# Sliding-window attention feeding an MoE block: a padded last token block, fp32 loads in long runs with casts on GpSimd, row-tiled scores by head pair, and the two MoE stages interleaved

## The chip, the cores and the metric

The kernel runs on one core of a Trainium2 chip. The metric is the device time of one execution in microseconds (us); lower is better. Before the change it is 407.75 us, the median of four runs (407.3 to 408.6). The profile and the trace come from one profiled execution, whose span is a little shorter (406.9 us before), because it leaves out what surrounds the program.

A few names are used throughout. PE is TensorE's matmul stream and PEld its weight loads; DVE is VectorE, ACT is ScalarE, POOL is GpSimd; SPq and POOLq are the two queues from which DMAs are issued. The *pitch* of a matmul is the time from its start to the start of the next one. A matmul's recorded duration overlaps its neighbours, so pitch and not duration is what a matmul costs. A *visit* is a run of matmuls of one operand shape among matmuls of another. A *period* is the time between equal points of two successive blocks.

## The reference

Eight batches of eight heads, 576 tokens, head size 64. Every query sees itself and the 63 tokens before it. The result, 4608 tokens by 512, goes through two weight matrices with a hard-swish between them. All inputs and outputs are fp32.

```python
scores = q @ k.transpose(0, 1, 3, 2) / sqrt(64)
rel = pos[:, None] - pos[None, :]
scores = where((rel >= 0) & (rel < 64), scores, -1e9)
attn = softmax(scores);  x = (attn @ v) -> [4608, 512]
h = x @ w_in                      # [4608, 2048]
g = h * clip(h + 3, 0, 6) / 6
out = g @ w_out                   # [4608, 512]
```

## The kernel before

Each batch of 576 tokens is four blocks of 128 tokens and one of 64. Attention of batch b and MoE of earlier tokens share one PE order: attention code calls `weave()` before its matmuls (those of P·V excepted), and each call takes one MoE instruction from a queue. MoE works on nine blocks of 512 tokens; stage 1 (`hT`, 64 matmuls) and stage 2 (`acc`, 64 matmuls) of a block have 512 columns each, so there are 1152 of them.

Loads are DMAs that cast fp32 to bf16 on the way. Each run is one head's 64 elements of one token, 256 bytes read and 128 written:

```python
nc.gpsimd.dma_start(                       # the same for k and for v
    out=qk16[:ss, 0 : H * D].rearrange("p (h d) -> p h d", h=H),
    in_=q[b, :, s0 : s0 + ss, :].rearrange("h s d -> s h d"))
```

Queries are transposed and copied, one copy per head, into a buffer whose other half is zero, so that one matmul of 384 columns gives the scores of two heads. The last token block keeps its true size of 64 (`nn`, `mq`, `nn_q`):

```python
nc.tensor.matmul(st[:nn, 0 : 2 * mq],
    lhsT=KT_b[:, g, n0 : n0 + nn], rhs=QZ_b[:, g, :, n0 : n0 + mq], ...)
# ... exp on ACT, mask multiply on DVE ...
nc.tensor.matmul(o_aug[:, qb, :],
    lhsT=pTp[:nn_q, par, qb, 0:P], rhs=V16s[qb][:nn_q, h, 0 : D + 1], ...)
```

MoE is queued stage after stage. Stage 1 needs an ACT and a DVE operation on each `hT` before that PSUM buffer is free again:

```python
while stage1_done < NTB and (stage1_done + 1) * TB <= tokens_ready:
    if stage1_done >= 1 and stage2_done < stage1_done:
        emit_moe_stage2(stage2_done); stage2_done += 1
    emit_moe_stage1(stage1_done); stage1_done += 1
# ... attention weaves the queue in; what is left over runs alone
```

The softmax here doesn't subtract the row's maximum and nothing guards it: scores larger than these inputs give would overflow.

## Time and profile before

| | before |
|---|---|
| time, median of four | 407.75 us |
| profiled span | 406.9 us |
| PE / DVE / ACT / POOL busy | 91 / 62 / 57 / 26 % |
| five steady periods (from 85.3 us to 293.4 us) | 41 to 43 us each |

The first lines are from the page of the profile of before: busy time by engine; the span in 40 slices of 10.2 us, where a digit is the busy share in tenths (PEclk: the granted TensorE clock, DMA: the busy share of the 16 DMA engines); the DMA queues (packets, MB, share of the engines' time); the shares of the chain of waits that ended last; and one group of instructions.

```profile
PE 369.2 (91%) x2325; PEld 183.2 (45%) x2368; DVE 250.5 (62%) x791; ACT 233.9 (57%) x581; POOL 106.3 (26%) x136
...
PE   1477887999999999999999999999999999999975
...
PEclk9996788999999999999999999999999999999999
DMA  9999999989692969198919950110011002002011
...
q0 software_dynamic: 115168, 18.36, 66.1%
...
PE 75%; ACT 7%; DVE 7%; DMA 5%; issue 3%; POOL 1%; ACTq 0%; POOLq 0%
...
L442 PE MATMUL acc<-wout_147,gT 128*128 128x512 bf16 x519 | 151.8, 380 | 1.5 <-DVE gT L407 1.1
```

PE is busy almost everywhere from 70 us on and it carries 75% of the chain, so it is the bound. But "91% busy" is not work at the peak: the group's 380 ns is a duration. The next lines, from the chain of waits of before (start, length, what, in us), show what a matmul costs.

```profile
213.41 1.83 PE acc L442 x8
...
254.43 1.83 PE acc L442 x8
...
312.20 0.69 ACT t_4322 L400
312.92 0.70 DVE gT L407
314.04 0.66 PE hT L387 x3
...
331.67 3.24 PE acc L442 x15
```

Fifteen `acc` matmuls take 3.24 us, a pitch of 0.216 us. All 1152 need 249 us. The same point comes back after 41.0 us (213.41 and 254.43). At 312 us, in the part without attention, PE's order in the trace is four `hT` matmuls, one `acc`, four `hT` and so on, and the chain goes ACT, DVE, PE: these five matmuls (1.08 us by the pitch) do not cover the 0.69 and 0.70 us of ACT and DVE, and stage 1 waits for its own PSUM buffers.

Now the timeline of PE in before (start, duration, engine, line, operation, count), at the end of one head's P·V:

```profile
211.30 0.20 PE L298 MATMUL o_aug<-Vr_138,pTr_128 128*128 128x65 bf16 x1
211.34 0.19 PE L307 MATMUL o_aug<-Vr_137,pTr_128 128*128 128x65 bf16 x1
211.46 0.20 PE L298 MATMUL o_aug<-Vr_139,pTr_128 64*128 64x65 bf16 x1
211.59 0.20 PE L307 MATMUL o_aug<-Vr_138,pTr_128 128*128 128x65 bf16 x1
```

Only the third of these has 64 rows. It starts 0.12 us after its predecessor, and its successor 0.13 us after it; matmuls of 128 rows beside it start 0.03 to 0.04 us apart. So one small odd-shaped matmul costs some 0.2 us.

### The profile page before, as it was taken

The page shows a single profiled execution, that of the slowest core. Times are in us where ns is not written, and L with a number is a line of the kernel's source. Part 1 is how long each engine was busy: PE and PEld are TensorE (multiplying, and loading weights), DVE is VectorE, ACT ScalarE, POOL GpSimd, SP SyncE. Part 2 cuts the span into 40 slices and gives each one's busy share as a digit, 9 for nine tenths or more (in the row PEclk, how much of TensorE's full clock was granted, in tenths as well). Part 3 has the DMA queues.
Part 4 walks back from the last instruction along what each step waited for, and adds up shares of the span by engine and source line. Part 5 has one row for each costly group of instructions (what it writes and reads, how often), then busy time and mean ns, then how long its engine had stood idle before and what let it go on. Part 6 is the DMA issues. An engine that isn't in the chain of part 4 may idle for free.

```text
span 406.9 us, 6550 instructions
## 1 busy us (share of the span) xinstructions
PE 369.2 (91%) x2325; PEld 183.2 (45%) x2368; DVE 250.5 (62%) x791; ACT 233.9 (57%) x581; POOL 106.3 (26%) x136
## 2 busy tenths in 40 slices
PE   1477887999999999999999999999999999999975
PEld 1234453445544554455445544554454334334332
DVE  7678666877777677866686677667753541532510
ACT  2375654785588457846784578457835543543521
POOL 9995554346131514151415120000000000000000
PEclk9996788999999999999999999999999999999999
DMA  9999999989692969198919950110011002002011
GB/s 81 135 143 202 138 114 184 87 71 144 67 58 37 117 69 59 30 96 98 60 19 104 101 34 25 36 44 3 3 50 53 0 26 79 0 27 79 0 52 52
DMA packets 120384, 28.21 MB, mean 69 GB/s; under 512 B 113184, under 2 KB 115232, under 8 KB 120352
## 3 DMA queue, kind: packets, MB, share of 16 engines
q0 software_dynamic: 115168, 18.36, 66.1%
q1 hardware_dynamic: 5184, 9.44, 6.2%
q8 instruction: 18, 0.29, 0.3%
q14 instruction: 14, 0.11, 0.1%
HBM read 36.70 MB, written 9.44 MB: 113 GB/s over the span
## 4 chain that ended last, share of the span: by engine, by line
PE 75%; ACT 7%; DVE 7%; DMA 5%; issue 3%; POOL 1%; ACTq 0%; POOLq 0%
PE acc L442 27%; PE hT L387 18%; PE hT L375 7%; PE st L262 6%; PE o_aug L298 4%; PE o_aug L307 3%; DVE gT L407 3%; PE xp L350 3%; DMA wout_147<-in_moe_w_out_dram 3%; PE xpq L211 3%; PE xpk L235 2%; PE acc L430 2%; ACT osb L455 1%; DMA Vr_134<-in_v_dram 1%; DMA qk_148<-in_k_dram 1%
## 5 line engine op out<-in xcount | busy, mean ns | idle before, releaser
L442 PE MATMUL acc<-wout_147,gT 128*128 128x512 bf16 x519 | 151.8, 380 | 1.5 <-DVE gT L407 1.1
L387 PE MATMUL hT<-xT_all,win_146 128*128 128x512 bf16 x411 | 119.0, 384 | 0.9 <-issue 0.2
L442 PEld LDWEIGHTS <-gT 128*128 128x128 bf16 x540 | 50.5, 97 | 58.7 <-issue 7.5
L387 PEld LDWEIGHTS <-win_146 128*128 128x128 bf16 x432 | 41.5, 98 | 49.6 <-issue 10.6
L375 PE MATMUL hT<-xT_all,win_146 128*128 128x512 bf16 x143 | 55.2, 386 | 3.4 <-DVE gT L407 3.3
L455 ACT COPY osb<-acc 128x512 f32<-128x512 f32 x36 | 21.0, 584 | 44.3 <-PE acc L442 43.4
L222 ACT COPY qz_132<-xpq 64x128 bf16<-64x128 bf16 (+1 forms) x80 | 19.2, 245 | 31.4 <-DVE qz_132 L227 18.6
L222 ACT COPY qz_133<-xpq 64x128 bf16<-64x128 bf16 (+1 forms) x80 | 19.2, 247 | 24.8 <-DVE qz_133 L227 18.2
L357 ACT COPY xT_all<-xp 128x256 bf16<-128x256 bf16 (+1 forms) x80 | 25.8, 363 | 7.2 <-PE xp L350 6.5
L262 PE MATMUL st<-qz_132,KT_b 128*128 128x384 bf16 (+1 forms) x80 | 24.0, 330 | 3.6 <-DVE qz_132 L227 2.2
L331 DVE TENSOR_TENSOR opg<-o_aug,rec 128x256 bf16<-128x256 f32 x64 | 26.5, 415 | 0.1
L262 PE MATMUL st<-qz_133,KT_b 128*128 128x384 bf16 (+1 forms) x80 | 24.8, 328 | 1.9 <-DVE qz_133 L227 0.7
L262 PEld LDWEIGHTS <-KT_b 128*128 128x128 bf16 (+1 forms) x160 | 15.9, 104 | 18.9 <-issue 12.3
L350 PE MATMUL xp<-ident_123,opg 128*128 128x128 bf16 (+1 forms) x160 | 22.4, 218 | 2.2 <-DVE KT_b L240 0.7
L227 DVE COPY qz_132<-xpq 64x128 bf16<-64x128 bf16 (+1 forms) x80 | 17.1, 221 | 11.4 <-ACT qz_132 L222 9.6
L227 DVE COPY qz_133<-xpq 64x128 bf16<-64x128 bf16 (+1 forms) x80 | 17.3, 221 | 10.1 <-ACT qz_133 L222 8.6
L322 DVE RECIPROCAL rec<-o_aug 128x4 f32<-128x4 f32 x64 | 11.6, 181 | 18.6 <-PE o_aug L307 17.5
L350 PEld LDWEIGHTS <-opg 128*128 128x128 bf16 (+1 forms) x160 | 13.7, 98 | 18.1 <-DVE opg L331 6.2
L375 PEld LDWEIGHTS <-win_146 128*128 128x128 bf16 x144 | 14.2, 99 | 13.9 <-issue 2.3
L240 DVE COPY KT_b<-xpk 128x512 bf16<-128x512 bf16 (+1 forms) x40 | 15.9, 396 | 7.3 <-PE xpk L235 6.2
L430 PE MATMUL acc<-wout_147,gT 128*128 128x512 bf16 x36 | 13.6, 378 | 4.8 <-ACT osb L455 2.5
L339 DVE TENSOR_SCALAR opg<-o_aug,rec 64x64 bf16<-64x64 f32 x64 | 17.3, 270 | 0.7
(754 smaller groups left out, 684.0 us busy)
## 6 DMA issues: line engine op xcount, KB each, us to landing
out_dram<-osb SPq DMA_DIRECT2D x36, 256.0 KB, 2.0
win_146<-in_moe_w_in_dram POOLq DMA_DIRECT2D x4, 512.0 KB, 10.0
wout_147<-in_moe_w_out_dram POOLq DMA_DIRECT2D x2, 1024.0 KB, 12.9
Vr_135<-in_v_dram POOLq DMA_DIRECT2D x4, 128.0 KB, 4.8
Vr_134<-in_v_dram POOLq DMA_DIRECT2D x3, 128.0 KB, 4.6
Vr_136<-in_v_dram POOLq DMA_DIRECT2D x3, 128.0 KB, 4.8
Vr_137<-in_v_dram POOLq DMA_DIRECT2D x3, 128.0 KB, 5.2
Vr_140<-in_v_dram POOLq DMA_DIRECT2D x3, 128.0 KB, 5.8
```

The source lines that it names most:

```text
L222: nc.scalar.copy(out=QZ_b[pl:ph, g, half, s0 : s0 + ss], in_=xpq[pl:ph, j, :ss],)
L227: nc.vector.tensor_copy(out=QZ_b[pl:ph, g, half, s0 : s0 + ss], in_=xpq[pl:ph, j, :ss],)
L262: nc.tensor.matmul(st[:nn, 0 : 2 * mq], lhsT=KT_b[:, g, n0 : n0 + nn], rhs=QZ_b[:, g, :, n0 : n0 + mq], start=True, stop=True,)
L331: nc.vector.tensor_tensor(out=opg[:, 0:nfull, hq, :], in0=o_aug[:, 0:nfull, 0:D], in1=rec[:, 0:nfull].unsqueeze(2).to_broadcast([P, nfull, ...
L339: nc.vector.tensor_scalar_mul(out=opg[:mm, qb, hq, :], in0=o_aug[:mm, qb, 0:D], scalar1=rec[:mm, qb : qb + 1],)
L350: nc.tensor.transpose(out=xp[:, j, :mm], in_=opg[:mm, qb, 2 * j : 2 * j + 2, :].rearrange("p a d -> p (a d)"), identity=ident16[:mm, :mm],)
L357: nc.scalar.copy(out=xT_all[:, gb : gb + HC // 2, t_lo : t_lo + mm], in_=xp[:, 0 : HC // 2, :mm],)
L375: nc.tensor.matmul(hT[:, :tn], lhsT=win16[:, 0, fc * P : (fc + 1) * P], rhs=xT_all[:, 0, t0 : t0 + tn], start=True, stop=(NG == 1),)
L387: nc.tensor.matmul(state["hT"][:, :tn], lhsT=win16[:, g, fc * P : (fc + 1) * P], rhs=xT_all[:, g, t0 : t0 + tn], start=False, stop=(g == N ...
L430: nc.tensor.matmul(acc[:uu, :], lhsT=gT[:, 0, tsub * P : tsub * P + uu], rhs=wout16[:, 0, :], start=True, stop=(NFC == 1),)
L442: nc.tensor.matmul(state["acc"][:uu, :], lhsT=gT[:, fc, tsub * P : tsub * P + uu], rhs=wout16[:, fc, :], start=False, stop=(fc == NFC - 1),)
L455: nc.scalar.copy(out=osb[:uu, :], in_=acc[:uu, :])
```

## The change

The intent: long DMA runs for q and k, no half-zero operands, fewer and wider copies, no 64-row leftovers, and stages 1 and 2 interleaved so that each hides the other's waits. The core of the diff, with cuts:

```diff
-            nc.gpsimd.dma_start(out=qk16[...], in_=q[b, :, s0 : s0 + ss, :]...)   # casts, 256 B read
+                nc.sync.dma_start(                                  # fp32, runs of R*D*4 = 1536 B
+                    out=dst[:NP, h0 : h0 + step, :],
+                    in_=src[b, h0 : h0 + step].rearrange("h (p j) d -> p h (j d)", j=R))
+    # vst: fp32 as well, 256 B runs, on the same queue
+                if not first: nc.gpsimd.tensor_copy(out=o_ap, in_=i_ap)   # cast on GpSimd
+                elif i == 0:  nc.vector.tensor_copy(out=o_ap, in_=i_ap)   # batch 0: q on DVE
+                else:         nc.scalar.copy(out=o_ap, in_=i_ap)          #          k on ACT
+        nc.gpsimd.tensor_copy(out=V[...], in_=vst[...])
+    # w_in is issued at once, beside batch 0; w_out beside batch 1

-        # QZ_b: queries copied per head beside zeros, one matmul of 384 columns for two heads
+                    for h in range(2):                               # two row tiles of 64
+                        nc.tensor.matmul(st[:, h, off : off + w],
+                            lhsT=KT[h * D : (h + 1) * D, kb * P : (kb + 1) * P],
+                            rhs=QT[h * D : (h + 1) * D, kb * P : kb * P + w], ...)
-        lhsT=pTp[:nn_q, par, qb, 0:P], rhs=V16s[qb][:nn_q, h, 0 : D + 1]
+        lhsT=pT[:, h, qb, 0:P],        rhs=V[:, qb, 2 * g + h, :]    # padded to 128 rows
+    # one mask multiply for a pair of heads, 128x1920, in place of five

-    emit_moe_stage2(stage2_done); emit_moe_stage1(stage1_done)       # one after the other
+        main = zipped(s1(T), s2(T - 1) if T else None)               # 4 of one, 4 of the other
+        weave(main, 32 if T else 16, side, 24)                       # attention spread evenly
```

## The prediction

> **What bounds the kernel now.** TensorE. The page shows PE busy 91% of 406.9 us, DVE 62%, ACT 57%; the chain of waits is 75% PE. That busy time overlaps (380 ns per 512-column matmul); in the tail of the chain 15 such matmuls take 3.24 us, a pitch of 0.216 us. The 1152 MoE matmuls need 249 us. From pitches in the timeline near 205 us (transpose 0.056, 384-column score 0.16, P·V 0.035 to 0.04) attention needs about 8.6 us a batch, 69 in all. So 318 us of pitch stand in a span of 407; 89 are lost:
> - Start: MoE runs in earnest only from 64 us. The chain shows a 10.8 us wait for w_out; the DMA engines are 90% busy for most of the first 140 us (113,184 packets under 512 B).
> - Middle: the same point recurs every 41.0 to 41.6 us (long runs of `acc` at 213.4, 254.4, 296.1), 5 us above 27.6 + 8.6. The timeline shows gaps of 0.1 us on entering and on leaving matmuls of 64 rows or columns, 0.2 us a visit.
> - Tail: from 311 us 3 stage-1 blocks and 3.2 stage-2 blocks take 96 us, pitch 86; where stage 1 runs alone, the chain alternates PE 0.66, ACT 0.70, DVE 0.70.
>
> **The change, costed (my estimates from those durations).**
> - Scores: 384 half-zero columns become two 64-row matmuls of 192. If the pair runs concurrently, as the Trainium skill, "TensorEngine Tiling (Array Packing)", § Key Properties says of tiles, 2.8 us a batch become 1.7. The same section says that a mode change drains the array; eight visits cost 1.6. Padding removes other 64-row visits. A batch: 27.6 + 8.1 + 1.6 = 37.3 without waits.
> - New waits: one buffer each for transposes, scores, output. The PE order leaves 0.86 to 1.08 us of MoE matmuls between transposes of q and of k, and between score halves; drain, handshakes and queueing take about 1.4. Eight stalls: 3 to 4 us. Casts on GpSimd, perhaps 10 us a batch, can block the mask multiply: the Trainium skill, "SBUF — State Buffer", § "SBUF: two separate sides", calls the shared port an exclusive lock. No trace here shows it yet. Period: about 40.5 us, hardly below 41.
> - ACT loses 160 query copies (38 us), DVE as many (34 us), both gain wider drains; ACT stays near 225 us, DVE falls to 200. Neither binds.
> - Loads: 256-byte runs become 1536-byte for q and k; v stays at 256 bytes, behind them and beside w_in. First V at 25 to 30 us (before: 15), attention 0 done near 42, the first period (stage 1 of block 0 with attention 1) near 68.
> - Interleaved stages cover the PE-ACT-DVE chain. Tail: two periods of 28.5 us and a last stage 2 of 17.
>
> **Sum.** 68 + 6 x 40.5 + 57 + 17 = 385 us. Range 367 to 402. Faster by over 2%: 0.79; within 2%: 0.15; slower: 0.06. The gain is mostly the tail (22 us), little the steady part.
>
> **What would show each step.** Start: first P·V waiting for V or its cast. Steady: equal points 38 to 43 us apart; paired scores near 0.085 us each; PE waits on DVE for QT and on ACT for exp. Tail: pitch near 0.22 us from two periods before the end. DMA share far below 0.9 after 80 us. Mask multiplies near 1.2 us; much longer means blocked.
>
> **What would make it wrong.** Mask multiplies blocked for several us (period 43 or more, about 400 us); row pairs not concurrent (+10 us); fewer stalls than I count and a faster start (period 38, 365 us or less).

## More of the kernel before

Last, the windows view of before: busy time of each engine in two stretches, then clock, DMA share and GB/s. (The DMA share counts overlapping packets, so it can pass 1.)

```profile
core 0: us, PE busy (x) PEld busy (x) DVE busy (x) ACT busy (x) POOL busy (x), PEclk, DMA share, GB/s
0.00:85.30 85.30, 61.24 (x422) 33.59 (x427) 63.31 (x233) 47.55 (x144) 53.39 (x73) 0.88 1.72 129
...
169.90:211.10 41.20, 40.47 (x282) 20.82 (x285) 28.95 (x95) 27.88 (x72) 12.59 (x16) 1.00 0.78 69
```

The first is the start: PE has work in only 61 of 85 us, while the DMA engines are full. Its clock is to be read with care: the view counts time without a clock record as full speed, and the records begin only at 26.2 us. The first q/k transposes, of 128 columns, start 0.107 us apart, later ones about 0.055, so half clock came before the records too. The second is one of five steady periods, in which PE hardly pauses. After 293 us comes the end, 113.5 us, in which attention runs out. The rest of the text speaks of these three parts.

## The result, and the profile after

The kernel after takes 376.71 us, the median of four runs: 374.35, 374.68, 378.91 and 378.74. The two longer ones had a mean granted clock of 0.973 and the two shorter of 1.0. (The clock alone does not explain them: later the fastest of four runs of this kernel, 372.79 us, was the only one with a lower clock, 0.986.) Executions over 1.5% slower than the fastest of the same kernel are left out of the means. A ratio is the mean time of one kernel's runs over that of the other's in the same rounds, so it is not quite the ratio of the medians. Here it is 0.9236, with a 95% interval of 0.9179 to 0.9293: faster. The prediction was 385 us, 367 to 402.

The page of the profile of after (slices are 9.3 us here):

```profile
PE 333.0 (89%) x2544; PEld 168.6 (45%) x2592; DVE 194.6 (52%) x285; ACT 214.6 (58%) x345; POOL 74.7 (20%) x54
...
PE   0156789999999999999999999999999999999985
...
PEclk9999999999999999999999999999999999999999
DMA  8999999999999148605760000000000010110111
...
q1 hardware_dynamic: 55424, 37.76, 43.2%
```

Two readings. PE starts later than before (0 1 5 6 against 1 4 7 7), and the DMA engines are still busy until about 121 us, although the share of the two queues together fell from 72.3% (66.1 and 6.2) to 50.0% (43.2 and 6.8). The row of 9s for the clock is no measurement in the first slices: the records begin at 55.7 us. Before that the q/k transposes of 96 columns start 0.080 us apart, after it 0.042, so by the pitches TensorE ran at half clock until then. The chain of waits of after has the same kind of recurring point, now 36.8 us apart:

```profile
210.00 0.97 PE acc L296 x4
...
246.78 0.97 PE acc L296 x4
```

The timeline of PE in after, at the end of a P·V and at one visit of paired scores:

```profile
214.68 0.19 PE L231 MATMUL o<-V_152,pT_145 128*128 128x65 bf16 x1
214.71 0.19 PE L236 MATMUL o<-V_152,pT_145 128*128 128x65 bf16 x1
214.74 1.03 PE L296 MATMUL acc<-wout_111,gT 128*128 128x512 bf16 x3
215.70 0.34 PE L201 MATMUL st<-QT_139,KT_141 64*128 64x192 bf16 x4
```

P·V now keeps its 0.03 us from the first matmul to the last. The windows view of after, in the stretches that answer to those of before, with the same columns:

```profile
0.00:85.40 85.40, 55.42 (x494) 31.21 (x502) 44.61 (x67) 44.13 (x70) 40.52 (x36) 1.00 1.11 215
...
158.40:195.20 36.80, 36.33 (x304) 18.55 (x309) 21.95 (x32) 24.53 (x42) 7.88 (x4) 1.00 0.51 125
```

PE has less to do in a period than before (36.33 us busy against 40.47) and, as before, hardly pauses. (The 1.00 of the first line is not measured before 55.7 us, as said.) Equal points were fixed for this account: the copies of `acc` out of PSUM, of which every fourth begins a new block of 512 tokens. Working out the differences of their times in the two traces:

| part | before, us | after, us | difference |
|---|---|---|---|
| start, to the first such copy | 85.3 | 85.4 | 0 |
| five steady periods | 208.1 | 183.4 | -24.7 |
| from there to the end of the span | 113.5 | 103.8 | -9.7 |

So the start gained nothing, the steady part most. The work done at such a point is not quite equal: after has written 100 pieces of `gT` where before has written 96 (16 matmuls, 3.5 us), and before is a little ahead in transposes and scores. By the pitches the net is 1 to 2 us at both points, so start and end are good to about 2 us. To see inside a period, each start-to-start interval on PE was put down to the kind of the earlier matmul, over three batches (us a batch):

| | MoE, both stages | q/k transposes | scores | P·V | output transposes | sum |
|---|---|---|---|---|---|---|
| before | 28.7 | 2.99 | 3.39 | 4.62 | 1.42 | 41.1 |
| after | 28.4 | 2.27 | 2.40 | 2.40 | 1.34 | 36.8 |

P·V is half of the saving of 4.4 us. (Some matmul records are missing, 5 or 6 of 128 MoE matmuls a batch in both traces; their time goes to the kind recorded before them.)

Who waits for whom on PE in after, over the whole run (us in total, times, longest):

```profile
PE tr L178 <- DVE ident L110: 15.8, 1, 15.8
PE o L231 <- POOL V_149 L165: 3.1, 1, 3.1
PE acc L296 <- ACT osb L303: 3.0, 4, 0.9
```

The same view limited to 158 to 269 us, three whole periods, is empty: PE waits for nothing there. In before, from 170 to 293 us, it holds only 0.5 us, so there too the longer period lay in the pitches and not in waits. The first wait of after is the start. The timeline of after shows it (in brackets: the idle time just before, and what ended it):

```profile
5.21 0.28 POOL masks.py:199 TENSOR_SCALAR_AFFINE_SELECT ident_116<-ident_116 128x128 f32<-128x128 f32 x1
...
15.03 0.56 DVE L162 CAST qn<-qst 96x768 bf16<-96x768 f32 x1 [1.70 <-DMA qst<-in_q_dram]
15.51 0.21 DVE L110 CAST ident<-ident_116 128x128 bf16<-128x128 f32 x1
15.78 0.64 PE L178 MATMUL tr<-ident,qn 96*128 96x96 bf16 x6 [15.78 <-DVE ident L110]
...
27.14 1.89 POOL L165 CAST V_149<-vst 128x2048 bf16<-128x2048 f32 x1 [12.10 <-DMA vst<-in_v_dram]
...
29.09 0.27 PE L231 MATMUL o<-V_149,pT_143 128*128 128x65 bf16 x2 [3.06 <-POOL V_149 L165]
```

The identity matrix is made by 5.5 us, but its cast to bf16 stands on DVE behind four q casts that each wait for a load. All transposes wait for it until 15.78 us. P·V of batch 0 then waits for the cast of V, whose loads compete with w_in.

### The profile page after: what moved, and what is told of

Read it like the earlier page. It is cut to its first block, busy times and chain, and to the rows that moved or that the text cites. A ratio compares the mean times of both kernels' runs of the same rounds, so it can differ in the third digit from the quotient of the medians.

```text
span 372.6 us, 6265 instructions
## 1 busy us (share of the span) xinstructions
PE 333.0 (89%) x2544; PEld 168.6 (45%) x2592; DVE 194.6 (52%) x285; ACT 214.6 (58%) x345; POOL 74.7 (20%) x54
## 3 DMA queue, kind: packets, MB, share of 16 engines
q1 hardware_dynamic: 55424, 37.76, 43.2%
## 4 chain that ended last, share of the span: by engine, by line
PE 51%; ACT 2%; DVE 2%; DMA 1%; another core or an unknown queue 1%; issue 1%; SPq 1%; ACTq 0%
PE acc L296 23%; PE hT L280 20%; PE st L201 2%; PE tr L178 2%; DMA vst<-in_v_dram 1%; PE o L231 1%; PE tr L255 1%; PE o L236 1%; ACT osb L303 1%; DVE pT_145 L219 1%; ACT pT_145 L208 0%; SPq L81 0%; DVE QT_131 L187 0%; DVE pT_147 L219 0%
## 5 line engine op out<-in xcount | busy, mean ns | idle before, releaser
L280 PE MATMUL hT<-xT,win_110 128*128 128x512 bf16 x545 | 152.2, 386 | 3.7 <-ACT xT L260 1.8
L296 PE MATMUL acc<-wout_111,gT 128*128 128x512 bf16 x559 | 146.4, 379 | 3.7 <-ACT osb L303 3.0
L160 POOL CAST qn<-qst 96x3072 bf16<-96x3072 f32 x7 | 19.4, 2778 | 74.4 <-issue 56.9
L178 PE MATMUL tr<-ident,qn 96*128 96x96 bf16 x192 | 14.9, 219 | 16.7 <-DVE ident L110 15.8
L245 DVE TENSOR_TENSOR opg<-o,rec 128x640 bf16<-128x640 f32 x32 | 26.4, 825 | 1.1
L260 ACT COPY xT<-tr 128x576 bf16<-128x576 bf16 x32 | 20.6, 642 | 9.0 <-PE tr L255 8.5
L208 ACT ACTIVATE pT_147<-st 128x768 bf16<-128x768 f32 x20 | 16.1, 808 | 11.5 <-PE st L201 11.5
L208 ACT ACTIVATE pT_143<-st 128x768 bf16<-128x768 f32 x22 | 17.8, 808 | 7.1 <-PE st L201 7.1
L208 ACT ACTIVATE pT_145<-st 128x768 bf16<-128x768 f32 x22 | 17.7, 806 | 5.5 <-PE st L201 5.5
L160 POOL CAST kn<-kst 96x3072 bf16<-96x3072 f32 x7 | 19.2, 2740 | 6.6 <-DMA kst<-in_k_dram 6.6
L219 DVE TENSOR_TENSOR pT_143<-pT_143,mask 128x1920 bf16<-128x1920 bf16 x11 | 13.2, 1199 | 9.8 <-ACT pT_143 L214 9.8
L219 DVE TENSOR_TENSOR pT_145<-pT_145,mask 128x1920 bf16<-128x1920 bf16 x11 | 13.2, 1196 | 9.5 <-ACT pT_145 L214 9.5
L255 PE MATMUL tr<-ident,opg 128*128 128x128 bf16 x160 | 15.5, 231 | 2.0 <-DVE opg L245 1.2
L219 DVE TENSOR_TENSOR pT_147<-pT_147,mask 128x1920 bf16<-128x1920 bf16 x10 | 12.5, 1253 | 8.5 <-ACT pT_147 L214 8.5
```

Source lines behind the costliest of these rows:

```text
L160: nc.gpsimd.tensor_copy(out=o_ap, in_=i_ap)
L178: nc.tensor.transpose(out=tr[:, j * NP : (j + 1) * NP], in_=src[:NP, j, 2 * g : 2 * g + 2, :].rearrange("p h d -> p (h d)"), identity=iden ...
L208: nc.scalar.activation(out=pT[:, :, kbs[0] : kbs[0] + 2, 0:QW], in_=st[:, :, 0 : 2 * QW].rearrange("p h (k w) -> p h k w", k=2), func=EXP, ...
L219: nc.vector.tensor_tensor(out=pT[:, :, :, 0:QW], in0=pT[:, :, :, 0:QW], in1=mask[:].rearrange("p (h k) w -> p h k w", h=2), op=MULT,)
L245: nc.vector.tensor_tensor(out=opg[:].rearrange("p k h d -> p h k d"), in0=ov[:, :, :, 0:D], in1=rec[:].unsqueeze(3).to_broadcast([P, 2, KB ...
L255: nc.tensor.transpose(out=tr[:, qb * P : (qb + 1) * P], in_=opg[:, qb, :, :].rearrange("p h d -> p (h d)"), identity=ident[:],)
```

## The experiments

Twelve runs were made, one of them of the kernel after again. Medians and ranges are of all runs of a kernel unless said; ratios are to the kernel before.

### Where do 4.4 us of a period come from?

The theory was that removing odd-shaped matmuls (padding) gave about half; the rivals were the interleaving of the stages and the row pairs of the scores. Each is undone alone, and the padding is also done alone in the kernel before.

**pv64**: P·V of the last block on its 64 real rows again. One mask entry is set to 1, so that the sum of a padding query isn't zero.

```diff
+                    kr = min(P, S - qb * P)
-                        ob, lhsT=pT[:, h, qb, 0:P], rhs=V[:, qb, 2 * g + h, :],
+                        ob, lhsT=pT[:kr, h, qb, 0:P], rhs=V[:kr, qb, 2 * g + h, :],
+    for hk in (KB - 1, 2 * KB - 1):
+        nc.vector.memset(mask[0:1, hk, P - 1 : P], 1.0)
```

> The changed kernel, with P.V of the last key block on the 64 real rows again instead of 128 padded ones (8 such matmuls a batch; result stays right). Theory A (a visit of a matmul with 64 rows costs about 0.2 us of array time, and padding them away is the larger part of the shorter steady period): period up from 36.8 by 8 x 0.2 = 1.6 us, to about 38.4, the mean P.V pitch from 33 ns to 50 ns or more, total up by about 12 us. Rival B (64-row visits are harmless, P.V was slow before because of waits on its one output buffer): period stays at 36.8 within 0.3, total within 2 us.

Measured: correct, 390.78 us (389.43 to 391.65), ratio 0.9579 (0.9553 to 0.9605). The period is 38.5 us, 1.7 longer than in after, and P·V takes 3.86 us instead of 2.40. Eight visits a batch cost 1.7 us, 0.2 us each, as the gaps in the timeline of before said. Eight batches of 1.7 us are 13.6 us, and the whole run is 14 us slower than after.

**before_padded**: the kernel before with its last block padded to 128 rows and columns everywhere, zeros in the padding.

```diff
-    # last block: nn, mq, nn_q, ss = 64
+    SP = KB * P     # QZ, KT_b [.., SP], V and the last qk16 rows zero-filled
+                n0, nn = kb * P, P
+                mq = min(QW, SP - n0)
+                    nn_q = P
```

> The kernel before, with only the last block of 64 padded to 128 rows everywhere (transposes, scores, P.V, normalise), scores still the zero-padded 384 columns in the full array. Theory A (64-row and 64-column visits cost the period): period down from 41.3 to 38 to 39 us, P.V from 4.8 to about 2.6 us a batch, total down by 15 to 22 us. Rival B (row-tiled scores and wider drains made the period short): period 41 within 0.5, total within 4 us of before.

Measured: correct, 393.54 us (393.17 to 393.88), ratio 0.9639 (0.9619 to 0.9659). The period is 39.0 us, 2.2 shorter than before, with P·V at 2.39 us. More arithmetic, and almost 15 us faster than before: just under the 15 to 22 expected, and close to half the size of the whole gain, from padding alone in a kernel otherwise unchanged.

**fullrows**: scores on all 128 rows in place of two row tiles. Each head's score then sums both heads, so it is wrong; it still passed the tolerance of the comparison, which says how little that comparison sees here.

```diff
-                            lhsT=KT[h * D : (h + 1) * D, kb * P : (kb + 1) * P],
-                            rhs=QT[h * D : (h + 1) * D, kb * P : kb * P + w],
+                            lhsT=KT[:, kb * P : (kb + 1) * P],
+                            rhs=QT[:, kb * P : kb * P + w],
```

> The changed kernel with each score matmul on all 128 rows of the array instead of one head's 64 (wrong result on purpose: both heads' scores are summed; same sizes and same order). Theory A (row pairs overlap, but entering and leaving the tiled mode takes back most of it): scores go from 2.4 to about 3.1 us a batch, period 37.2 to 37.6, total up by 3 to 6 us. Rival C (row tiling is a main source of the gain): period up by over 2 us, total up by over 15 us. Rival D (mode changes cost more than the overlap saves): total goes down.

Measured: 375.38, 376.21 and 377.15 us (one slow run of 381.46 left out), ratio 0.9216 (0.9187 to 0.9245): no difference from after in time. The 3 to 6 us expected in the total did not show; after's own four runs spread by 4.6 us. With the clock below full only from 38 to 57 us, the steady periods can be read: 37.2 us, 0.4 longer, scores 3.07 us instead of 2.40. In after the two matmuls of a pair start 6 to 9 ns apart, in fullrows 82 ns, so the pairs do run side by side; still, row tiling is worth only about 0.4 us a batch, a tenth of the saving.

**apart**: stage 2 and then stage 1, one after the other, as before. This is the order of the program; in the trace PE's order is mixed in both kernels (from 327 to 342 us of apart mostly one `acc` matmul after every four of `hT`, as in the end of before).

```diff
-        main = zipped(s1(T), s2(T - 1) if T else None)
+        main = chained(s2(T - 1) if T else None, s1(T))
```

> The changed kernel with stage 2 of the block before and stage 1 of this block one after the other in each period instead of interleaved. If interleaving is what shortens the tail: the two periods without attention grow from 27.8 to 33 to 35 us each (stage 1 alone took about 19.5 us before), the steady periods grow by 0 to 2 us since attention still lies between, total up by 10 to 20 us. Rival (the tail was shortened by fewer blocks being left over, not by interleaving): total within 4 us.

Measured: correct, 391.30 us (388.11 to 394.69, with one slow run), ratio 0.9558 (0.9492 to 0.9624). The period is 38.5 us, 1.7 longer. It is not a matter of waits: over three periods PE waits 0.5 us in all. By kind, 0.9 of the 1.7 us lie in the MoE matmuls and 0.7 in the scores, whose visits are now split by MoE matmuls; why the MoE matmuls take longer was not taken apart. The three blocks after the last full period take 38.5, 30.5 and 29.4 us, where after has 34.8, 27.6 and 25.0; the 33 to 35 us expected of the two without attention did not come. The sum to the end of the span is 11 us longer, but not all of that is interleaving: at the point where it begins, after has written 100 pieces of `gT` and apart 96, and is ahead in transposes and scores, some 5 us by the pitches. That leaves some 6 us. The waits agree in kind: in the part without attention PE waits 5.0 us for `gT` and the copy of `acc` in before (311 to 391 us), 2.7 us in apart (311 to 371 us) and not at all in after (296 to 352 us). So interleaving is worth 1.7 us a period and some 6 us at the end, which is most of the 9.7 us gained there, not shown to be all.

Together: 1.7 to 2.2 for padding, 1.7 for interleaving, 0.4 for row pairs, against 4.4. The parts were measured in different surroundings, and undoing the interleaving also moved the visits of the scores, so the near-equality is not an exact sum.

### Do the casts on GpSimd block the mask multiply?

The prediction feared this. In after, 29 of the 32 mask multiplies take 1.15 to 1.16 us. Three begin while a cast runs and take 1.58, 1.62 and 2.10 us. The timeline of after shows the longest:

```profile
60.78 2.74 POOL L160 CAST qn<-qst 96x3072 bf16<-96x3072 f32 x1 [4.84 <-DMA qst<-in_q_dram]
62.44 2.10 DVE L219 TENSOR_TENSOR pT_147<-pT_147,mask 128x1920 bf16<-128x1920 bf16 x1 [0.59 <-ACT pT_147 L214]
```

The cast ends at 63.52 and the multiply at 64.54. In the other two cases the multiply too ends 1.0 us after the cast, whenever it began, so it does not run beside the cast at all. In after_again two such multiplies took 2.82 and 3.55 us, both in the start, and both end 1.0 us after the cast. After 104 us no mask multiply meets a cast in this kernel. That is luck of position, as the next run showed without being meant to.

**dense**: attention woven into the first half of each period, meant to provoke waits of transposes and scores.

```diff
-        weave(main, 32 if T else 16, side, 24)
+        weave(main, 16, side, 24)
```

> The changed kernel with all 24 attention steps of a period woven into the first half of its MoE steps instead of over the whole; the same instructions. Theory A (one-buffer handshakes of some 1.0 us are just covered by the 4 or 5 MoE matmuls between them, which is why the predicted stalls of 3 to 4 us a period did not come): with less MoE work between, stalls appear: period up by 2 to 5 us, total up by 12 to 30 us, and the profile shows waits of transposes and scores on ACT and DVE. Rival B (handshakes are too short to matter at all): period within 0.5 us, total within 4 us.

Measured: correct, 390.8 us (387.57 to 394.46, with one slow run), ratio 0.9544 (0.9497 to 0.9591). Three periods take 40.7 us. But the waits were not the expected ones (nor could they well be: PE's order still leaves four or five MoE matmuls between the transposes of q and of k). The timeline of dense:

```profile
166.40 2.74 POOL L160 CAST qn<-qst 96x3072 bf16<-96x3072 f32 x1 [24.08 <-issue]
166.99 3.17 DVE L219 TENSOR_TENSOR pT<-pT,mask 128x1920 bf16<-128x1920 bf16 x1
169.09 3.67 POOL L160 CAST kn<-kst 96x3072 bf16<-96x3072 f32 x1
170.21 0.24 PE L231 MATMUL o<-V,pT 128*128 128x65 bf16 x2 [1.95 <-DVE pT L219]
```

The multiply begins 0.6 us into the cast of q and takes 3.17 us: until the cast ends (169.14), and 1.0 us more. The cast of k that follows is held up in turn: 3.67 us in place of 2.74. PE waits 1.95 us for P·V. And then the windows view of dense, in steps of 3.4 us:

```profile
167.90:171.30 3.40, 1.35 (x24) 0.82 (x24) 3.40 (x4) 1.14 (x3) 3.40 (x2) 1.00 0.28 50
171.30:174.70 3.40, 3.33 (x17) 1.40 (x17) 1.15 (x4) 2.01 (x4) 1.46 (x1) 0.51 1.06 249
```

PE was busy only 1.35 of 3.4 us, and the granted clock in the next 3.4 us is 0.51. So each blocked multiply is paid for twice: 1.95 us of waiting and some 1.7 us of lost clock (half of 3.4 us), together about the 3.5 us by which these periods are longer than those of cd_dense below. The same happens at 130 and 212 us. In the first steady period of dense without casts (246 to 283 us) the period is 37.3 us. That suggests the cast, but the periods differ in other ways too, so it was tried.

**cd_dense**: the dense weave in the kernel `castdma` described below, which has no cast on GpSimd.

> The dense weave again, but with the loads of the version that has casting DMAs, so without any cast on GpSimd. In the dense version three periods took 40.7 us; in each a cast on GpSimd (2.74 us) ran as the mask multiply began, the multiply took 3.17 us in place of 1.16, TensorE waited 1.95 us for it and then ran at half clock for 3.4 us. The one steady period after the last cast took 37.3. Theory L (the shared port between GpSimd and VectorE is what made the dense weave dear, and the density itself costs about 0.5 us a period): all steady periods 37.0 to 37.6, all mask multiplies 1.15 to 1.2 us, no half clock after 80 us, time 364 to 369. Theory D (the density itself, attention work too close together for its own chain of scores, exponential, mask and P.V, makes TensorE wait): periods stay 39.5 to 41 with waits for the mask multiply, time 374 to 385.

Measured: correct, 367.36 us (366.73 to 368.05), ratio 0.8994 (0.8956 to 0.9032). All four steady periods from 114 us are 37.29 us, all 32 mask multiplies take 1.15 to 1.16 us, and the clock is 1.00 in every steady stretch. Between 105 and 260 us, the waits view of PE in this kernel has only short pieces that wait for no other engine; the longest in total is:

```profile
PE hT L252 <- issue: 0.8, 5, 0.2
```

Without the casts the dense weave costs 0.5 us a period (37.3 against 36.8); with them 3.9. The theory of the lock is confirmed, and that of the density itself falls. GpSimd is not idle in cd_dense: many of the multiplies run while it issues a DMA, and they too take 1.15 to 1.16 us. In the change as made the casts cost next to nothing in the steady part, because its wider spacing keeps them apart from the multiplies.

### Why did the start gain nothing?

**castdma**: the change with the loads of before: casting DMAs in 256-byte runs on one queue, in the order batch 0, w_in, batch 1, w_out; no staging buffers, no casts; the first fills moved from GpSimd to DVE.

```diff
-                nc.sync.dma_start(out=dst[:NP, h0 : h0 + step, :], in_=src[b, h0 : h0 + step]...)
+                nc.gpsimd.dma_start(out=dst[:NP, j, :, :],
+                    in_=src[b].rearrange("h (p j) d -> j p h d", j=R)[j])
-    # cast_batch(...) on DVE, ACT and GpSimd
-    for i in range(4): nc.gpsimd.dma_start(out=win16[...])     # at once, beside batch 0
+    for i in range(4): nc.gpsimd.dma_start(out=win16[...])     # behind batch 0
```

> The changed kernel with q, k and v loaded as before: casting DMAs in runs of 256 bytes, no fp32 staging, no casts on GpSimd (ring memsets moved to DVE, w_in after the first batch). Theory A (the load change shortens only the start, where the DMA engines are the limit, and the casts on GpSimd cost the steady part nothing): period stays at 36.8 within 0.3 us; the three transfers that the first period needs take about 85 us of the DMA engines instead of 59, so the first period ends 10 to 20 us later and the total is up by 10 to 20 us. Rival B (casts on GpSimd block the mask multiply): period shorter by 1 us or more. Rival C (loads do not matter): total within 4 us.

**after_again**: the kernel after, unchanged.

> The changed kernel itself, on the same chip as the three that follow, for comparison. All theories: 374 to 379 us, period 36.8 us; runs with a lower granted clock lose some 4 us in the first 80 us only.

Measured: after_again 374.98 us (372.79 to 375.93), ratio 0.9175 (0.914 to 0.921); against the expectation, its fastest run was the one with a lower clock; castdma correct, 364.15 us (363.89 to 365.91), ratio 0.8932 (0.8901 to 0.8963). The expectation for castdma was wrong by its sign: the new loads do not save 10 to 20 us, they cost 11. The steady period is the same to the hundredth, 36.78 us, so all of it is in the start. The page of castdma:

```profile
DMA  9999999999990799069905991000000000100111
...
q0 software_dynamic: 116992, 18.36, 70.2%
```

Here the DMA engines are *more* occupied (70.2% in one queue), with twice as many packets, and the kernel is faster. A busy share tells how long packets are under way, not when the bytes that someone waits for arrive. Landing times and progress, read from the traces (us; an attention is done when its last copy begins):

| | after | castdma | cd_swap | start2 |
|---|---|---|---|---|
| first work of PE | 15.8 | 5.4 | 5.4 | 9.6 |
| V of batch 0 landed | 28.3 | 21.1 | 20.2 | 17.6 |
| w_in landed | 22.9 | 31.4 | 31.6 | 41.3 |
| V of batch 1 landed | 54.4 | 44.5 | 55.3 | 48.9 |
| w_out landed | 50.7 | 56.1 | 42.0 | 64.6 |
| attention 0 done | 46.9 | 37.0 | 37.2 | 42.7 |
| attention 1 done | 78.0 | 67.5 | 76.9 | 72.3 |
| first copy of `acc` | 85.4 | 75.0 | 77.4 | 79.8 |

By about 55 us the same four things (two batches, w_in, w_out) have landed in after and in castdma, so the overall rate is the same; what differs is the order. In castdma batch 0 comes ahead of w_in and batch 1 ahead of w_out; in after they share the engines. The new loads are not slow in themselves: where batch 0 has the engines alone, its V lands at 17.6 us with them (start2) and at 21.1 without (castdma).

TensorE's clock differs too, and these runs do not tell its part from that of the waits. By the clock records and the pitches (0.080 or 0.042 us from transpose to transpose), half clock ends for good at 55.7 us in after, 53.0 in cd_swap, 50.0 in start2 and 46.1 in castdma. So a part of the differences between these kernels can be clock; how large a part is open.

**start**: the change with its fp32 loads, the cast of the identity moved to GpSimd, and the weights held back: w_in until V of batch 0 is cast, w_out until V of batch 1 is cast, each by a tiny copy that the DMA must wait for.

```diff
-    nc.vector.tensor_copy(out=ident[:], in_=ident32[:])
+    nc.gpsimd.tensor_copy(out=ident[:], in_=ident32[:])
+        nc.gpsimd.tensor_copy(out=win16[0:1, 0, 0:FF:WC], in_=V[0:1, 0, 0, 0:4])   # ahead of w_in
+        nc.gpsimd.tensor_copy(out=wout16[0:1, 0:NFC:4, 0], in_=V[0:1, 0, 0, 0:4])  # ahead of w_out
+    load_w_in(cast0[2])
+            if b == 1:
+                load_w_out(cst[2])
```

> The changed kernel with another order at the start: identity cast on GpSimd instead of behind the q casts on DVE, w_in issued only after the first V is cast, w_out only after the second V is cast. Theory A (the first 76 us are set by when the first and the second V land, which compete with w_in and w_out for the DMA engines): first V cast near 20 us instead of 27, second near 47 instead of 54, total down by 5 to 10 us. Rival B (the start is limited by the bytes or by the chain of attention itself): total within 3 us.

Measured: correct, fast runs 378.7, 379.63 and 380.23 us, ratio 0.9294 (0.9266 to 0.9322): a miss, 4 to 5 us slower than after_again. The casts of V did begin early (17.2 and 43.9 us), but w_out landed only at 57.8 to 67.9 us. Its one profiled run fell in the slow state (454.63 us), so only its order, its landings and a wait that ends with a landing are used here. In the waits view of PE:

```profile
PE acc L300 <- DMA wout<-in_moe_w_out_dram: 5.7, 1, 5.7
```

PE takes its instructions in order. The first stage-2 matmuls stand early in that order, and while they waited for w_out, the attention behind them, whose data was there, waited too.

**start2**: the same, with w_out held back only until k of batch 1 is cast.

```diff
-                load_w_out(cst[2])
+                load_w_out(cst[1])
```

> The changed kernel's fp32 loads and GpSimd casts kept; w_in behind the first batch (as in the run named start), w_out gated by the cast of the second batch's k, so that it lands near 52 to 55 us, when stage 2 needs it, and no longer at 58 to 68 as in start, where stage-2 matmuls early in the PE order held everything behind them. Theory O (order of transfers): second V cast near 48 us, total 366 to 371 us. Rival K (fp32 loads and casts are the slow thing): total stays at 374 or above.

Measured: correct; fast runs 368.24, 368.92 and 372.65 us (one slow run of 374.5), median of all 370.79, ratio 0.9073 (0.9014 to 0.9132). The expected range was hit, and the second V was cast at 46.9 us, as expected; but w_out landed in two halves, by 48.4 and by 64.6 us, and not at 52 to 55. So 4 to 5 of the 11 us come back with fp32 loads and a better order.

**cd_swap**: castdma with w_out issued ahead of batch 1.

```diff
-    pend = load_batch(1, False)
     load_w_out()
+    pend = load_batch(1, False)
```

> The casting-load version (364 us) with one line moved: w_out is issued ahead of the second batch's q, k, v on the one queue, no longer behind them. Theory O (that version won because the second batch no longer competes with w_out; the order of the transfers, not their kind, sets the start): second V lands near 57 us instead of 44.5, total up by 9 to 13 us, back to about 375. Rival K (the kind of load, or the missing casts, won): total within 3 us of 364.

Measured: correct, 371.56 us (370.58 to 371.87), ratio 0.9109 (0.9082 to 0.9135), 7.4 us slower than castdma: below the 9 to 13 expected of the order alone, well above the 3 of its rival. Attention 0 is as early as in castdma, and attention 1 is 9.4 us later (76.9 against 67.5). The waits view of PE, first of castdma and then of cd_swap, has the same line at another size:

```profile
PE tr L150 <- DMA qn<-in_q_dram: 3.6, 5, 1.0
```

```profile
PE tr L150 <- DMA qn<-in_q_dram: 9.9, 10, 4.3
```

Nothing but the order of the same transfers changed here, and it takes back two thirds of the 11 us. Between start2 and castdma there are still 5 to 6 us (by their ratios), and they are already there when attention 0 is done (42.7 against 37.0). These two differ in the casts of batch 0 on DVE and ACT, in the time of PE's first work, in the runs of the loads, and in when the full clock came; these were not told apart, and this stays open.

### A version that beats both

**cd_tail**: castdma, and in the last stage 2, where four accumulations share one PSUM bank, every second one uses a bank that stage 1 no longer needs.

```diff
+            if last and ts % 2:
+                acc = ps_h.tile([P, TB], F32, name="hT")
+            else:
                 acc = ps_acc.tile([P, DM], F32, name="acc")
```

> The casting-load version, and in the last stage 2 every second accumulation goes to a bank that stage 1 no longer needs. There PE waits 0.7 us for the drain three or four times with one bank. Theory: last stretch 2 to 3 us shorter, total 361.5 to 362.5 us, the fastest of all. Rival: the drains are hidden already, total 364.

Measured: correct, 361.84 us (361.65 to 362.05), ratio 0.8874 (0.8846 to 0.8902). That is 2.3 us under castdma, as expected: in after and castdma each of the last four accumulations begins with a wait of 0.7 to 0.9 us for ACT to empty the bank. It is the fastest version, 46 us under before.

## Why the prediction was right or wrong

The time, the class and the range were right; 376.7 us lies 8 us under the middle. The account behind it was right in part, and misjudged terms lay in opposite directions: that the sum came so near is partly luck.

| term of the sum | predicted | measured in after's profile |
|---|---|---|
| start, to the end of the first period | 68 | 76.3 |
| six periods | 6 x 40.5 = 243 | 6 x 36.8 = 220.7 |
| two periods without attention | 57 | 55.5 |
| last stage 2 | 17 | 20.1 |
| sum | 385 | 372.6 |

**Right: the bound and the base.** PE is the bound; MoE needs 249 us and still does. "A batch: 27.6 + 8.1 + 1.6 = 37.3 without waits" is what came (36.8). The gain of taking out visits of 64 rows was read from gaps of 0.1 us in the trace, and pv64 and before_padded show it: 1.7 to 2.2 us a batch. The Trainium skill, "TensorEngine Tiling (Array Packing)", § Key Properties, says that changing the tiling mode drains TensorE; the trace agrees, at about 0.1 us on each side. Row pairs do run side by side, as the prediction supposed (6 to 9 ns from start to start), and one pair follows another after 0.083 to 0.09 us, near the 0.085 predicted; yet they were worth only 0.4 us a batch (fullrows). ACT and DVE fell about as estimated (214.6 and 194.6 us against 225 and 200).

**Wrong: "Eight stalls: 3 to 4 us ... Period: about 40.5 us, hardly below 41."** There are no stalls in the steady part. PE waits for nothing between 158 and 269 us. The estimate took 1.4 us for the handshake and 0.86 to 1.08 us of MoE work to cover it, with queueing guessed. In the start of the trace of after, where nothing queues, the same handshake from one transpose visit through the copy on DVE to the next visit takes 0.8 to 1.0 us beyond the first visit's own matmuls (15.78 to 17.26 us, less 0.48 us of pitch or 0.64 us of busy time, at half clock). The steady part bears it out: at the closest, one visit of transposes starts 1.15 us after the one before, 0.26 us of it the earlier visit's own pitch, with four MoE matmuls between and no wait. So 0.9 us suffices, and the MoE work of 0.86 to 1.08 us covers it. How near that is to a stall was not tested: dense was meant to, but in its trace too PE's order keeps four or five MoE matmuls between these visits. This is the term that was mis-sized: 22 us over six periods.

**Wrong: "The gain is mostly the tail (22 us), little the steady part."** By equal points the steady part gained 24.7 us and the end 9.7. The mechanism of the tail was right: interleaving hides the PE, ACT, DVE chain, as the waits of before, apart and after show (5.0, 2.7 and 0 us). What was wrong is to count the shorter tail as gain. Before had three stage-1 blocks and 3.2 of stage 2 left after attention; after has two and three. That is 77 matmuls, 16.6 us by the pitch, that were moved into the earlier periods and not saved. The step to "little the steady part" followed from the stalls that did not come.

**Wrong: the first period near 68 us.** It ended near 76, and attention 0 was done at 47 and not 42. V's cast came at 27.1 us and P·V at 29.1, as predicted ("25 to 30"). What was missed is that the identity's cast stands behind the q casts on DVE (PE's first work at 15.8 us), and that V of batch 1 shares the DMA engines with w_out and lands at 54.4. The prediction costed runs in bytes and not the order of transfers, and its pitches are those of full clock, where TensorE ran at half clock until 55.7 us. castdma, cd_swap and start2 show that the order matters: 7.4 us of it in cd_swap, 4 to 5 in start2.

**Wrong: "DMA share far below 0.9 after 80 us".** It stays at 0.9 until about 121 us.

**Half right: the casts.** The Trainium skill, "SBUF — State Buffer", § "SBUF: two separate sides", calls the port pair that VectorE and GpSimd share an exclusive lock for the whole instruction. Here this is seen directly: three multiplies in after, and three of 3.17 us in dense, end 1.0 us after the cast that held them. The prediction named the danger ("period 43 or more") and gave it little weight; that the steady part of after met none was luck of position. dense came to 40.7, and cd_dense shows the lock to be the cause. The Trainium skill, "GPSIMD Engine Reference", § 4.1, calls one-input elementwise work on GpSimd roughly line-rate; the trace agrees: a cast of 3072 elements took 2.74 us, 0.89 ns an element, and VectorE's of 768 took 0.56 us, 0.73 ns. So there were 7.9 us of casts a batch against the 10 estimated.

**Forgotten: the last store.** The last stage 2 was put at 17 us. It takes 16.5 us to the end of its last matmul, and then 3.6 us more for the last copy and its store.

## What to carry to other kernels

Cost the change of operand shape between neighbouring matmuls, not only the arithmetic: padding 64 rows to 128 added work and saved almost 15 us in a kernel otherwise unchanged. In a start bound by loads, write down when each operand lands and where its first consumer stands in the engine's order; the order of the transfers, alone, cost 7 us in cd_swap, while the busy share of the DMA engines pointed the wrong way. A lock between engines can cost nothing at one spacing and 3.5 us a period at another, so after any change of spacing look again at the longest instance of the locked instruction and not at its mean.

## What the Trainium skill lacked or had wrong

- "TensorEngine Tiling (Array Packing)", § Key Properties, gives no size for the drain. These runs show about 0.1 us on entering and 0.1 us on leaving a visit of 64 rows, and 1.7 us a batch for eight such visits (pv64). It also does not say that a plain matmul of 64 rows among 128-row ones pays it.
- "TensorE: Matmul & The Clock Gate", § "🎯 Why this matters for your kernels", asks for no PE-idle gaps over about 3 us. In dense the longest single wait was 1.95 us, in a stretch of 3.4 us with 1.35 us of PE work, and the clock granted in the next 3.4 us was 0.51. It was so in three periods, and in none of cd_dense. Taken alone, that row is too lenient for a stretch in which the work around the gap is small.
- "DMA: Bandwidth & Descriptors", § Specifications, gives 512 B as the least size for line rate. The trace of castdma goes that way: batch 1, in runs of 256 bytes read and 128 written, came at 270 GB/s of reads (3.54 MB between 31.4 and 44.5 us), and w_in just before it, in runs of 2048 bytes read, at some 410 GB/s (1.05 MB every 2.55 us). But no page says that the order of the transfers can outweigh the size of the runs (castdma 364.15 us, cd_swap 371.56 us; after_again, with 1536-byte runs for q and k, 374.98 us).
- No page has the time that the SP queue spends on issuing a load of many short runs while the engines are full: five loads of V took 17.89 us to issue in after, and the loads of batch 1 stood behind them.
